# Products with the high and the low half of an input as one matmul, in three layers of an expert kernel

## The chip, the cores and the metric

One NeuronCore of a Trainium2 chip runs the whole program. The metric is device time in microseconds (us). The kernel before took 526.72 us, the median of three runs (526.52 to 526.78).

## The reference

The program is linear attention followed by a mixture of 16 experts. Only the second half matters here. Every token (4608 of them, 512 numbers each) goes to one expert, and there

```python
h = np.maximum(xg[mask_e] @ w1[g, e], 0.0)
ye = h @ w2[g, e]
out[tok_idx] = combined[:, None] * ye
```

with `w1` of 512 x 1024 and `w2` of 1024 x 512 for each of the 16 experts, all in float32. Run on the reference's inputs, the three smallest experts get 246, 238 and 217 tokens.

## The kernel before, in words

The experts are sorted by their number of tokens and worked off one after the other as regions r = 0 to 15. Tokens stand in the columns of a matmul's moving operand, weights are stationary. A region has a list of widths (`ARMS`, line 22); at run time TensorE branches to the smallest width that holds the region's tokens (`by_width`, line 337), and `CAPS` is the largest. The operations of ScalarE, VectorE and GpSimd always cover `CAPS[r]` columns, or whole groups of 32 (`groups_of`).

To keep float32 accuracy at the matmul's fast rate, every operand is split in a high part (rounded) and a low part (the rest), and a product is three matmuls (`three`, line 369): high weight by high input, high weight by low input, low weight by high input, all added up in one PSUM bank. Layer 1 of a region has 8 groups (f = 0 to 7), each of 4 chunks c by three matmuls, 96 in all; layer 2 has 4 groups (d = 0 to 3), each of 8 chunks by three, also 96. The layers of all regions follow each other on TensorE. Region 15 is the last; its layer 2 has tokens as stationary and weights as moving operand (`layer2_by_token`, line 1445) and starts with 24 matmuls of 512 columns, which read all of w2.

Around the matmuls the other engines work in an order that is written out by hand (`manual_schedule`, line 1460): each engine does its instructions strictly in the order of the code. In layer 1 of region r:

- after each group f, ScalarE takes the relu of the bank as the high part hh, and VectorE the low part hl (`split_h`, lines 324 and 325). Four banks go round, so group f + 4 waits for hl of group f;
- a quarter of w1 and four pieces of w2 are split: ScalarE rounds the high part (lines 246 and 348), VectorE subtracts for the low part (lines 250 and 352). The last quarter of w1 goes ahead of group f = 1, the pieces 0 to 3 of w2 ahead of f = 0, 2, 4 and 6 (`w1_at`, `w2_at`, line 1632);
- at f = 0, GpSimd is given the scaling of the next region's tokens (line 321, it reads and writes SBUF) and one indirect DMA for each group of 32 columns of the region before (line 1439). In region 15 these DMAs stand behind all of layer 1's code, as does `gpsimd.drain()`.

In layer 2, for each d, VectorE transposes the next region's tokens (line 311), ScalarE rounds them (line 1431), VectorE takes their low part (line 1435); three quarters of the next w1 are split (lines 246 and 250); and VectorE transposes the result of the bank psy[d] into z (line 1655).

Of the kernel before, what the change touches and what calls it, by code (L numbers as in the profile page):

```python
# [9 lines left out]
F32 = mybir.dt.float32  # L10
F32R = mybir.dt.float32r
# [3 lines left out]
ALU = mybir.AluOpType  # L15
# [5 lines left out]

ARMS = [[128], [336, 344, 360], [328, 336, 344], [312, 328], [304, 312, 328], [300, 312], [300, 304],
        [292, 300], [280, 292], [284, 292], [268, 280], [272, 280], [264, 268],
        [248, 264], [240, 260], [232, 256]]
CAPS = [arms[-1] for arms in ARMS]


# [5 lines left out]
XO = 20  # L33
XR = 18
QUICK = [0, 1, 2, 3, 4, 5, 6, 7]


PICK = 1
# [29 lines left out]
def tile_linattn_moe(ctx: ExitStack, tc: tile.TileContext, qm, qt, k, v, router, w1, w2, out):  # L68
# [179 lines left out]
    def split_low(part, h, eng):  # L248
        w, hi, lo = quarter(part, h)
        eng.tensor_tensor(out=lo, in0=w, in1=hi.bitcast(F32), op=ALU.subtract)  # L250
# [72 lines left out]
    def split_h(hh, hl, ps):  # L323
        nc.scalar.activation(out=hh, in_=ps, func=AF.Relu)  # L324
        nc.vector.scalar_tensor_tensor(out=hl, in0=ps, scalar=0.0, in1=hh.bitcast(F32), op0=ALU.max, op1=ALU.subtract)  # L325

    def layer1(ps, w1, f, xh, xl, n):
        cs = slice((f % 4) * P, (f % 4 + 1) * P)
        _, wh, wl = w1[f // 4]
        three(ps[:, 0:n], KC, lambda c: wh[:, c, cs], lambda c: wl[:, c, cs], lambda c: xh[:, c, 0:n],  # L330
              lambda c: xl[:, c, 0:n])

    def columns(r, engine):
        return nc.values_load(ncol[0:1, r:r + 1], engines=[engine], min_val=ARMS[r][0], max_val=CAPS[r],
# [2 lines left out]
    def by_width(n, choices, emit):  # L337
        if len(choices) == 1:
            emit(choices[0])
            return  # L340
        with tc.If(n <= choices[0]) as arm:
            emit(choices[0])
        with arm.Else():
            by_width(n, choices[1:], emit)
# [2 lines left out]
        hf, i2 = p // 2, p % 2  # L347
        nc.scalar.copy(out=piece(hi, hf, i2), in_=halfpiece(wt[hf][0], i2))  # L348

    def split2_low(wt, hi, lo, p):  # L350
        hf, i2 = p // 2, p % 2
        nc.vector.tensor_tensor(out=piece(lo, hf, i2), in0=halfpiece(wt[hf][0], i2),  # L352
                                in1=piece(hi, hf, i2).bitcast(F32), op=ALU.subtract)

    def piece(x, hf, i2):
        return x[:, :, :, 64 * hf + 32 * i2:64 * hf + 32 * (i2 + 1)]

    def halfpiece(w, i2):
        return w[:, :, P * i2:P * (i2 + 1)].rearrange("p c (j x) -> p c j x", x=32)
# [9 lines left out]
    def three(ps, n, stat_h, stat_l, mov_h, mov_l, lo=0, hi=None, late=0):  # L369

        hi = n if hi is None else hi
        rest = list(range(lo, lo + late))
        for c in range(lo, hi):
            nc.tensor.matmul(ps, lhsT=stat_h(c), rhs=mov_h(c), start=(c == 0), stop=False)  # L374
            nc.tensor.matmul(ps, lhsT=stat_h(c), rhs=mov_l(c), start=False, stop=False)  # L375
            if c < lo + late - 1:
                continue
            for d in rest or [c]:
                nc.tensor.matmul(ps, lhsT=stat_l(d), rhs=mov_h(d), start=False, stop=(d == n - 1))  # L379
            rest = []  # L380
# [932 lines left out]
    with ExitStack() as ph:  # L1313
# [105 lines left out]
            return idx  # L1419

        def new_x(r):
            return [mp.tile([P, KC, 384], F32R, name=nm, bufs=1)[:, :, 16 * FIRST_X[r]:] for nm in ("xh", "xl")]

        def turned(r, c):
            n = groups_of(r)
# [1 line left out]
            turn_x(xt[:, 0:32 * n], xqs[r % 2], n, c)  # L1427
            return xt

        def split_high_x(xh, xt, r, c):  # L1430
            nc.scalar.activation(out=xh[:, c, 0:CAPS[r]], in_=xt[:, 0:CAPS[r]], func=AF.Copy, scale=g2[:, 0:1])  # L1431

        def split_low_x(x, xt, r, c):
            xh, xl = (y[:, c, 0:CAPS[r]] for y in x)
            nc.vector.scalar_tensor_tensor(out=xl, in0=xt[:, 0:CAPS[r]], scalar=g2[:, 0:1], in1=xh.bitcast(F32),
                                           op0=ALU.mult, op1=ALU.subtract)

# [42 lines left out]
        HALF = KC * FF // 2  # L1480
        la = mp.tile([P, 2 * HALF], F32R, name="la", tag="w2h", bufs=1)
        lb = mp.tile([P, 2 * HALF], F32R, name="lb", tag="w2l", bufs=1)
        lc = mp.tile([P, FC * 384], F32R, name="lc", tag="hh", bufs=1)
        ld = mp.tile([P, FC * 384], F32R, name="ld", tag="hl", bufs=1)
        w1r = [(w1c[hf], *(x.rearrange("p (c f) -> p c f", c=KC) for x in y)) for hf, y in enumerate((
            (lc[:, 0:HALF], ld[:, 0:HALF]), (la[:, HALF:2 * HALF], lb[:, HALF:2 * HALF])))]
        xT, xTl = (lb[:, i * DM:(i + 1) * DM].rearrange("p (c t) -> p c t", c=KC) for i in range(2))
# [56 lines left out]
        for hf in range(2):  # L1544
            ps = bank()
            for c in range(KC):
                if hf == 1 and c == 2:
                    xts = [turned(1, i) for i in range(2)]
                    turn(0)
                    for i in range(2):  # L1550
                        split_high_x(x1[0], xts[i], 1, i)
                    split_low_x(x1, xts[0], 1, 0)
                    xts.append(turned(1, 2))
                    split_low_x(x1, xts[1], 1, 1)
                    w1n.append(half_layer(ev, 0, 1))
                three(ps, KC, lambda c: xT[:, c, :], lambda c: xTl[:, c, :], lambda c: w1r[hf][1][:, c, :],
                      lambda c: w1r[hf][2][:, c, :], lo=c, hi=c + 1)
            nc.scalar.activation(out=hr[:, hf * 512:(hf + 1) * 512], in_=ps, func=AF.Relu)
# [4 lines left out]
        turn(1)  # L1563
        xts.append(turned(1, 3))
        for i in range(2, 4):
            split_high_x(x1[0], xts[i], 1, i)
        split_low(w1n[0], 0, nc.vector)
        for i in range(2, 4):
            split_low_x(x1, xts[i], 1, i)
# [27 lines left out]
        for r in range(1, NE):  # L1597
            cap, n = CAPS[r], groups_of(r)
            last = r + 1 == NE
            xh, xl = cur  # L1600
            hh = mp.tile([P, FC, 384], F32R, name="hh", tag="hh", bufs=1)[:, :, 16 * FIRST_H[r]:]
            hl = mp.tile([P, FC, 384], F32R, name="hl", tag="hl", bufs=1)[:, :, 16 * FIRST_H[r]:]
            w2h = mp.tile([P, FC, 4, P], F32R, name="w2h", tag="w2h", bufs=1)
            w2l = mp.tile([P, FC, 4, P], F32R, name="w2l", tag="w2l", bufs=1)
            nw1 = nw2 = None
            width_r = columns(r, mybir.EngineType.PE)
            for f in range(FC):
                if f in w1_at:
                    split_piece(w1c, w1_at[f])
                if f in w2_at:  # L1610
                    split2_high(w2c, w2h, w2_at[f])
                    split2_low(w2c, w2h, w2l, w2_at[f])
                ps = bank()
                by_width(width_r, ARMS[r], lambda m: layer1(ps, w1c, f, xh, xl, m))
                split_h(hh[:, f, 0:cap], hl[:, f, 0:cap], ps[:, 0:cap])
                if r > 1:
                    next(tables, None)
                    next(tables, None)
                elif f == 4:
                    idx = indices(1)  # L1620
                if f == FC - 1 and last:
                    nc.gpsimd.drain()
                if f == 0 and not last:
                    scale(r + 1)
                    if r > 1:
                        for g in range(groups_of(r - 1)):
                            put_quarters(z, zidx, g)
                if f == 1 and not last:
                    nw1, nw2 = load_weights(eidx[0:1, r + 1:r + 2])
                if f == 2 and r + 2 < NE:  # L1630
                    pass
            w1_at, w2_at = {1: 3}, {0: 0, 2: 1, 4: 2, 6: 3}
            if last:
                for g in range(groups_of(r - 1)):
                    put_quarters(z, zidx, g)
                nc.vector.scalar_tensor_tensor(out=ridx[:, 1:3], in0=rid[:, 1:3], scalar=0.25, in1=bad[0][:, 1:3],
                                               op0=ALU.mult, op1=ALU.max)
                layer2_by_token(r, (w2h, w2l), hh, hl, ridx[:, 1:3])
                break
            z = mp.tile([P, NQ, P], F32, name="z")  # L1640
            nxt = new_x(r + 1)
            zidx = idx
            xt = [turned(r + 1, 0)]
            for d in range(4):
                split_high_x(nxt[0], xt[d], r + 1, d)
                if d < 3:
                    split_high(nw1[d // 2], d % 2)
                    xt.append(turned(r + 1, d + 1))
                    split_low(nw1[d // 2], d % 2, nc.vector)
                split_low_x(nxt, xt[d], r + 1, d)  # L1650
                ps = psy[d]
                by_width(width_r, ARMS[r], lambda m: three(
                    ps[:, 0:m], FC, lambda c: w2h[:, c, d, :], lambda c: w2l[:, c, d, :], lambda c: hh[:, c, 0:m],
                    lambda c: hl[:, c, 0:m]))
                nc.vector.transpose(z[:, 0:n, 32 * d:32 * (d + 1)], ps[:, 0:32 * n])
            idx = indices(r + 1)
            if r + 3 <= NE:
                read(r + 2) if r + 2 < NE else None
            cur, w1c, w2c = nxt, nw1, nw2
# [115 lines left out]
```

## Time and profile before

| | |
|---|---|
| median of the runs shown | 526.72 us |
| the profiled execution's own time | 526.29 us |
| its span, first to last instruction | 524.5 us |
| regions 1 to 15 on TensorE | 138.0 to 519.1 us |
| region 13, layers 1 and 2 (248 columns) | from 453.75, 464.64 us |
| region 14, layers 1 and 2 (240 columns) | from 475.51, 486.24 us |
| region 15, layers 1 and 2 (232 columns, then 512 and 256) | from 497.00, 507.71 us |

How to read it: the profile is one execution, with times from the span's start. A matmul's record shows its whole way through the engine, some 0.27 to 0.40 us, and the next one starts long before it ends, so the cost of one matmul in a stream is the distance from its start to the next start. Names such as `ps<-xl,whi` say which tile is written from which. PE is TensorE, PEld its weight loads, DVE is VectorE, ACT is ScalarE, POOL is GpSimd.

### The profile page before, as it was taken

How to read it: one execution, taken by the hardware profiler on the slowest of the kernel's cores; microseconds unless marked ns; L12 is line 12 of the kernel's file. 1: busy time of each engine (PE TensorE's matmuls, PEld its weight loads, DVE VectorE, ACT ScalarE, POOL GpSimd, SP SyncE). 2: the span in 40 equal slices, each digit the busy share in tenths (PEclk: the TensorE clock that was granted, in tenths of full speed). 3: DMA queues.
4: the chain of work that ended last, by engine and by line, in shares of the span. 5: the costliest groups of instructions: out<-in, count | busy, mean ns of one | idle time of the engine just before them, and what ended most of it. 6: DMA issues, size and time to landing. Idle time of an engine off the chain costs nothing. (4 is left out here: it accounts for less than half of the span.)

```text
span 524.5 us, 12156 instructions
## 1 busy us (share of the span) xinstructions
PE 512.8 (98%) x4258; PEld 496.4 (95%) x4262; DVE 400.9 (76%) x853; ACT 277.9 (53%) x499; POOL 258.4 (49%) x356
## 2 busy tenths in 40 slices
PE   6899999999999999999999999999999999999995
PEld 3899998689999999999999999999999999999995
DVE  4259998978888887887777777877878777878760
ACT  0377888725753544455454454545453656456451
POOL 7002865452112736647484646555564738265271
PEclk9899999999999999999999999999999999999999
DMA  8999998947897483636765656564748384864010
GB/s 319 422 422 419 418 423 345 363 176 244 263 373 311 114 322 95 267 104 196 279 232 188 230 190 242 181 262 152 280 140 318 104 335 131 305 213 179 15 40 36
DMA packets 44026, 126.50 MB, mean 241 GB/s; under 512 B 6992, under 2 KB 26390, under 8 KB 32925
## 3 DMA queue, kind: packets, MB, share of 16 engines
q1 hardware_dynamic: 36029, 105.71, 54.7%
q0 software_dynamic: 7760, 19.48, 10.0%
q8 instruction: 62, 1.02, 0.8%
q14 instruction: 31, 0.25, 0.2%
q10 hardware_dynamic: 144, 0.04, 0.0%
HBM read 105.73 MB, written 20.51 MB: 241 GB/s over the span
## 5 line engine op out<-in xcount | busy, mean ns | idle before, releaser
L1439 POOL DMA_INDIRECT out_dram<-z,idx x140 | 163.9, 1171 | 152.6 <-DVE idx L1417 105.4
L379 PE MATMUL ps<-xh,wlo 128*128 128x300 f32 (+12 forms) x480 | 141.5, 295 | 0.0
L374 PE MATMUL ps<-xh,whi 128*128 128x300 f32 (+12 forms) x480 | 141.3, 294 | 0.0
L375 PE MATMUL ps<-xl,whi 128*128 128x300 f32 (+12 forms) x480 | 141.2, 294 | 0.0
L374 PE MATMUL psy<-hh,w2h 128*128 128x300 f32 (+11 forms) x448 | 132.4, 296 | 0.0
L375 PE MATMUL psy<-hl,w2h 128*128 128x300 f32 (+11 forms) x448 | 132.4, 296 | 0.0
L379 PE MATMUL psy<-hh,w2l 128*128 128x300 f32 (+11 forms) x448 | 132.4, 295 | 0.0
L250 DVE TENSOR_TENSOR wlo<-wr,whi 128x1024 fp32r<-128x1024 f32 x64 | 97.2, 1521 | 21.2 <-ACT whi L246 21.1
L375 PEld LDWEIGHTS ps<-xl,whi 128*128 128x128 f32 x480 | 90.4, 188 | 0.0
L374 PEld LDWEIGHTS ps<-xh,whi 128*128 128x128 f32 x480 | 90.3, 188 | 0.0
L379 PEld LDWEIGHTS ps<-xh,wlo 128*128 128x128 f32 x480 | 90.3, 188 | 0.0
L324 ACT ACTIVATE hh<-ps 128x328 fp32r<-128x328 f32 (+11 forms) x120 | 50.4, 420 | 74.2 <-PE ps L379 66.9
L352 DVE TENSOR_TENSOR w2l<-wr,w2h 128x1024 fp32r<-128x1024 f32 x60 | 73.4, 1223 | 17.3 <-ACT w2h L348 16.6
L374 PEld LDWEIGHTS psy<-hh,w2h 128*128 128x128 f32 x448 | 84.2, 188 | 0.0
L375 PEld LDWEIGHTS psy<-hl,w2h 128*128 128x128 f32 x448 | 84.2, 188 | 0.0
L379 PEld LDWEIGHTS psy<-hh,w2l 128*128 128x128 f32 x448 | 84.1, 188 | 0.0
L348 ACT CAST w2h<-wr 128x1024 fp32r<-128x1024 f32 x60 | 62.5, 1042 | 37.1 <-PE psy L375 34.0
L325 DVE SCALAR_TENSOR_TENSOR hl<-ps,hh 128x328 fp32r<-128x328 f32 (+11 forms) x120 | 55.6, 464 | 21.0 <-ACT hh L324 20.9
L1431 ACT ACTIVATE xh<-xt,rw 128x328 fp32r<-128x328 f32 (+11 forms) x60 | 32.5, 544 | 67.7 <-DVE xt L311 67.7
L246 ACT CAST whi<-wr 128x1024 fp32r<-128x1024 f32 x64 | 66.2, 1037 | 0.0
L267 POOL DMA_INDIRECT xs<-xo,keys x36 | 35.7, 993 | 31.3 <-DVE pt L762 10.3
L609 PE MATMUL ops<-kvx,m_q 128*128 128x168 f32 x256 | 42.2, 315 | 0.2 <-ACT xr L552 0.2
(304 smaller groups left out, 666.8 us busy)
## 6 DMA issues: line engine op xcount, KB each, us to landing
wr<-in_w_dram SPq DMA_DIRECT2D x64, 1024.0 KB
m_q<-in_qm_dram SPq DMA_DIRECT2D x8, 1024.0 KB
m_k<-in_k_dram SPq DMA_DIRECT2D x7, 1024.0 KB
m_v<-in_v_dram SPq DMA_DIRECT2D x7, 1024.0 KB
xq<-xs SPq DMA_DIRECT2D x20, 153.0 KB
out_dram<-z,idx POOLq DMA_INDIRECT x140
xq<-xs SPq DMA_DIRECT2D x16, 136.0 KB
xq<-xs SPq DMA_DIRECT2D x12, 119.0 KB
```

The costliest lines, as they stand in the source:

```text
L246: nc.scalar.copy(out=hi, in_=w)
L250: eng.tensor_tensor(out=lo, in0=w, in1=hi.bitcast(F32), op=ALU.subtract)
L267: sc = nc.gpsimd.indirect_dma_start(out=xs, out_offset=bass.IndirectOffsetOnAxis(ap=keys[:, c:c + 1], axis=0), in_=x.rearrange("p i f -> p ...
L324: nc.scalar.activation(out=hh, in_=ps, func=AF.Relu)
L325: nc.vector.scalar_tensor_tensor(out=hl, in0=ps, scalar=0.0, in1=hh.bitcast(F32), op0=ALU.max, op1=ALU.subtract)
L348: nc.scalar.copy(out=piece(hi, hf, i2), in_=halfpiece(wt[hf][0], i2))
L352: nc.vector.tensor_tensor(out=piece(lo, hf, i2), in0=halfpiece(wt[hf][0], i2), in1=piece(hi, hf, i2).bitcast(F32), op=ALU.subtract)
L374: nc.tensor.matmul(ps, lhsT=stat_h(c), rhs=mov_h(c), start=(c == 0), stop=False)
L375: nc.tensor.matmul(ps, lhsT=stat_h(c), rhs=mov_l(c), start=False, stop=False)
L379: nc.tensor.matmul(ps, lhsT=stat_l(d), rhs=mov_h(d), start=False, stop=(d == n - 1))
L609: nc.tensor.matmul(ops[c][lo:hi, pr, 0:XW], lhsT=qs[:, pr * step_ + at + lo:pr * step_ + at + hi], rhs=kx[:, pr, :], start=True, stop=True)
L1439: sc = nc.gpsimd.indirect_dma_start(out=out4, out_offset=bass.IndirectOffsetOnAxis(ap=idx[:, g:g + 1], axis=0), in_=z[:, g, :], in_offset= ...
```

## The change

In layer 2 of regions 13 and 14 and in layer 1 of region 15 (`PAIRED`), the high weight is multiplied with the input's high and low part in one matmul of 2m columns, where m is the region's width. It writes two halves of a bank, from column 0 and from column 256; the low weight's matmul of m columns is added to the first half. The sum of the halves is then made by ScalarE, which copies the second half to SBUF, and VectorE, which adds the copy to the first half in place. In region 15 the relu and its low part of group f - 1 are issued between the copy and the addition of group f. The tiles of the high and the low input become one tile of two halves, for all regions. The last three regions' widths change: the largest is now 256, and the smaller one of region 15 is 220 (232 before). Four of VectorE's subtractions are given to GpSimd: two in `LOW_1` (w1, layer 2 of regions 13 and 14, at d = 1) and two in `LOW_2` (w2 pieces 0 and 2, region 15). Once, in region 2, the part of the four psy banks that nothing has written is set to zero.

```diff
         [292, 300], [280, 292], [284, 292], [268, 280], [272, 280], [264, 268],
-        [248, 264], [240, 260], [232, 256]]
+        [248, 256], [240, 256], [220, 256]]
 CAPS = [arms[-1] for arms in ARMS]
...
 QUICK = [0, 1, 2, 3, 4, 5, 6, 7]
+
+
+PAIRED = {(13, 2), (14, 2), (15, 1)}
+LOW_2 = {(15, 0), (15, 2)}
+LOW_1 = {(13, 1), (14, 1)}
...
-    def layer1(ps, w1, f, xh, xl, n):
+    def layer1(ps, w1, f, x, n, pair):
         cs = slice((f % 4) * P, (f % 4 + 1) * P)
         _, wh, wl = w1[f // 4]
-        three(ps[:, 0:n], KC, lambda c: wh[:, c, cs], lambda c: wl[:, c, cs], lambda c: xh[:, c, 0:n],
-              lambda c: xl[:, c, 0:n])
+        products(ps, n, KC, lambda c: wh[:, c, cs], lambda c: wl[:, c, cs], x, pair)
+
+    def products(ps, m, n, stat_h, stat_l, x, pair):
+
+        if not pair:
+            three(ps[:, 0:m], n, stat_h, stat_l, lambda c: x[:, 0, c, 0:m], lambda c: x[:, 1, c, 0:m])
+            return
+        both_parts = ps.rearrange("p (i t) -> p i t", i=2)[:, :, 0:m]
+        for c in range(n):
+            nc.tensor.matmul(both_parts, lhsT=stat_h(c), rhs=x[:, :, c, 0:m], start=(c == 0), stop=False)
+            nc.tensor.matmul(ps[:, 0:m], lhsT=stat_l(c), rhs=x[:, 0, c, 0:m], start=False, stop=(c == n - 1))
+
+    def copy_low(ps, at, cap):
+        nc.scalar.copy(out=at, in_=ps[:, 256:256 + cap])
+
+    def add_low(ps, at, cap):
+        nc.vector.tensor_tensor(out=ps[:, 0:cap], in0=ps[:, 0:cap], in1=at, op=ALU.add)
...
-    def split2_low(wt, hi, lo, p):
+    def split2_low(wt, hi, lo, p, eng):
         hf, i2 = p // 2, p % 2
-        nc.vector.tensor_tensor(out=piece(lo, hf, i2), in0=halfpiece(wt[hf][0], i2),
+        eng.tensor_tensor(out=piece(lo, hf, i2), in0=halfpiece(wt[hf][0], i2),
                                 in1=piece(hi, hf, i2).bitcast(F32), op=ALU.subtract)
...
         def new_x(r):
-            return [mp.tile([P, KC, 384], F32R, name=nm, bufs=1)[:, :, 16 * FIRST_X[r]:] for nm in ("xh", "xl")]
+            return mp.tile([P, 2, KC, 384], F32R, name="x", bufs=1)[:, :, :, 16 * FIRST_X[r]:]
...
-        def split_high_x(xh, xt, r, c):
-            nc.scalar.activation(out=xh[:, c, 0:CAPS[r]], in_=xt[:, 0:CAPS[r]], func=AF.Copy, scale=g2[:, 0:1])
+        def split_high_x(x, xt, r, c):
+            nc.scalar.activation(out=x[:, 0, c, 0:CAPS[r]], in_=xt[:, 0:CAPS[r]], func=AF.Copy, scale=g2[:, 0:1])
         def split_low_x(x, xt, r, c):
-            xh, xl = (y[:, c, 0:CAPS[r]] for y in x)
+            xh, xl = (x[:, i, c, 0:CAPS[r]] for i in range(2))
             nc.vector.scalar_tensor_tensor(out=xl, in0=xt[:, 0:CAPS[r]], scalar=g2[:, 0:1], in1=xh.bitcast(F32),
...
         lb = mp.tile([P, 2 * HALF], F32R, name="lb", tag="w2l", bufs=1)
-        lc = mp.tile([P, FC * 384], F32R, name="lc", tag="hh", bufs=1)
-        ld = mp.tile([P, FC * 384], F32R, name="ld", tag="hl", bufs=1)
+        lcd = mp.tile([P, 2, FC * 384], F32R, name="lcd", tag="h", bufs=1)
+        lc, ld = lcd[:, 0], lcd[:, 1]
         w1r = [(w1c[hf], *(x.rearrange("p (c f) -> p c f", c=KC) for x in y)) for hf, y in enumerate((
...
                     for i in range(2):
-                        split_high_x(x1[0], xts[i], 1, i)
+                        split_high_x(x1, xts[i], 1, i)
                     split_low_x(x1, xts[0], 1, 0)
...
         for i in range(2, 4):
-            split_high_x(x1[0], xts[i], 1, i)
+            split_high_x(x1, xts[i], 1, i)
         split_low(w1n[0], 0, nc.vector)
...
             last = r + 1 == NE
-            xh, xl = cur
-            hh = mp.tile([P, FC, 384], F32R, name="hh", tag="hh", bufs=1)[:, :, 16 * FIRST_H[r]:]
-            hl = mp.tile([P, FC, 384], F32R, name="hl", tag="hl", bufs=1)[:, :, 16 * FIRST_H[r]:]
+            h = mp.tile([P, 2, FC, 384], F32R, name="h", tag="h", bufs=1)[:, :, :, 16 * FIRST_H[r]:]
+            hh, hl = h[:, 0], h[:, 1]
+            pair1, pair2 = ((r, i) in PAIRED for i in (1, 2))
             w2h = mp.tile([P, FC, 4, P], F32R, name="w2h", tag="w2h", bufs=1)
...
                     split2_high(w2c, w2h, w2_at[f])
-                    split2_low(w2c, w2h, w2l, w2_at[f])
+                    split2_low(w2c, w2h, w2l, w2_at[f], nc.gpsimd if (r, w2_at[f]) in LOW_2 else nc.vector)
                 ps = bank()
-                by_width(width_r, ARMS[r], lambda m: layer1(ps, w1c, f, xh, xl, m))
-                split_h(hh[:, f, 0:cap], hl[:, f, 0:cap], ps[:, 0:cap])
+                by_width(width_r, ARMS[r], lambda m: layer1(ps, w1c, f, cur, m, pair1))
+                if pair1:
+                    low = mp.tile([P, 384], F32, name="xt", bufs=3)[:, 0:cap]
+                    copy_low(ps, low, cap)
+                    if f:
+                        split_h(*behind)
+                    add_low(ps, low, cap)
+                    behind = (hh[:, f, 0:cap], hl[:, f, 0:cap], ps[:, 0:cap])
+                    if f == FC - 1:
+                        split_h(*behind)
+                else:
+                    split_h(hh[:, f, 0:cap], hl[:, f, 0:cap], ps[:, 0:cap])
                 if r > 1:
...
             for d in range(4):
-                split_high_x(nxt[0], xt[d], r + 1, d)
+                split_high_x(nxt, xt[d], r + 1, d)
                 if d < 3:
                     xt.append(turned(r + 1, d + 1))
-                    split_low(nw1[d // 2], d % 2, nc.vector)
+                    split_low(nw1[d // 2], d % 2, nc.gpsimd if (r, d) in LOW_1 else nc.vector)
                 split_low_x(nxt, xt[d], r + 1, d)
                 ps = psy[d]
-                by_width(width_r, ARMS[r], lambda m: three(
-                    ps[:, 0:m], FC, lambda c: w2h[:, c, d, :], lambda c: w2l[:, c, d, :], lambda c: hh[:, c, 0:m],
-                    lambda c: hl[:, c, 0:m]))
+                by_width(width_r, ARMS[r], lambda m: products(
+                    ps, m, FC, lambda c: w2h[:, c, d, :], lambda c: w2l[:, c, d, :], h, pair2))
+                if pair2:
+                    low = z[:, 0:n, 32 * d:32 * (d + 1)]
+                    nc.scalar.copy(out=low, in_=ps[:, 256:256 + cap].rearrange("p (n x) -> p n x", x=32))
+                    nc.vector.tensor_tensor(out=ps[:, 0:cap].rearrange("p (n x) -> p n x", x=32),
+                                            in0=ps[:, 0:cap].rearrange("p (n x) -> p n x", x=32), in1=low, op=ALU.add)
                 nc.vector.transpose(z[:, 0:n, 32 * d:32 * (d + 1)], ps[:, 0:32 * n])
+                if r == 2:
+                    nc.vector.memset(ps[:, 384:512], 0.0)
             idx = indices(r + 1)
```

## Rows read from the trace of the kernel before

**Rows 1.** The page, part 1: busy time, share of the span and instructions of each engine

```profile
PE 512.8 (98%) x4258; PEld 496.4 (95%) x4262; DVE 400.9 (76%) x853; ACT 277.9 (53%) x499; POOL 258.4 (49%) x356
```

**Rows 2.** The waits of PE, the longest of all: us in total, times, longest

```profile
PE warm L458 <- POOL wide_b L116: 2.2, 1, 2.2
```

**Rows 3.** Busy time of each engine in three paired layers

```profile
464.60:475.50 10.90, 10.90 (x98) 10.90 (x97) 9.45 (x17) 5.17 (x8) 3.84 (x3) 1.00 0.93 352
...
486.20:497.00 10.80, 10.80 (x99) 10.80 (x99) 8.48 (x17) 5.15 (x8) 1.97 (x2) 1.00 0.04 12
...
497.00:507.70 10.70, 10.70 (x98) 10.70 (x97) 8.65 (x13) 7.45 (x12) 7.61 (x8) 1.00 0.13 40
```

**Rows 4.** Timeline of PE: start, duration; first matmuls of late layers

```profile
464.64 0.27 PE L374 MATMUL psy<-hh,w2h 128*128 128x248 f32 x1
...
475.51 0.27 PE L374 MATMUL ps<-xh,whi 128*128 128x240 f32 x1
...
486.24 0.27 PE L374 MATMUL psy<-hh,w2h 128*128 128x240 f32 x1
...
497.00 0.27 PE L374 MATMUL ps<-xh,whi 128*128 128x232 f32 x1
...
507.71 0.40 PE L374 MATMUL psy<-w2h,hh 128*128 128x512 f32 x1
...
507.95 0.42 PE L375 MATMUL psy<-w2l,hh 128*128 128x512 f32 x1
...
513.22 0.28 PE L374 MATMUL psy<-w2h,hh 128*128 128x256 f32 x1
```

**Rows 5.** Timeline of PE: first matmuls of region 1, both layers, and region 2

```profile
138.04 0.33 PE L374 MATMUL ps<-xh,whi 128*128 128x360 f32 x1
...
154.03 0.33 PE L374 MATMUL psy<-hh,w2h 128*128 128x360 f32 x1
...
169.40 0.31 PE L374 MATMUL ps<-xh,whi 128*128 128x336 f32 x1
```

**Rows 6.** Timeline of ACT in region 15

```profile
505.51 1.04 ACT L348 CAST w2h<-wr 128x1024 fp32r<-128x1024 f32 x1
...
506.57 0.39 ACT L324 ACTIVATE hh<-ps 128x256 fp32r<-128x256 f32 x1
...
516.29 0.37 ACT L1456 COPY yo<-psy 128x256 f32<-128x256 f32 x1 [2.29 <-PE psy L379]
```

**Rows 7.** Timeline of DVE in region 15, layer 1

```profile
499.95 1.23 DVE L250 TENSOR_TENSOR wlo<-wr,whi 128x1024 fp32r<-128x1024 f32 x1 [0.18 <-ACT whi L246]
...
501.09 0.42 DVE L325 SCALAR_TENSOR_TENSOR hl<-ps,hh 128x256 fp32r<-128x256 f32 x1
...
501.43 1.22 DVE L352 TENSOR_TENSOR w2l<-wr,w2h 128x1024 fp32r<-128x1024 f32 x1
...
506.59 1.23 DVE L352 TENSOR_TENSOR w2l<-wr,w2h 128x1024 fp32r<-128x1024 f32 x1 [0.51 <-ACT w2h L348]
```

**Rows 8.** Timeline of POOL and DVE where both are busy, regions 1 and 13

```profile
143.01 0.52 DVE L325 SCALAR_TENSOR_TENSOR hl<-ps,hh 128x360 fp32r<-128x360 f32 x1
...
143.02 2.57 POOL L321 TENSOR_TENSOR xq<-xq 128x1408 f32<-128x1408 f32 x1 [0.62 <-DMA xq<-xs]
...
143.44 3.23 DVE L250 TENSOR_TENSOR wlo<-wr,whi 128x1024 fp32r<-128x1024 f32 x1
...
466.82 1.94 POOL L321 TENSOR_TENSOR xq<-xq 128x1024 f32<-128x1024 f32 x1
...
467.72 2.13 DVE L250 TENSOR_TENSOR wlo<-wr,whi 128x1024 fp32r<-128x1024 f32 x1 [1.22 <-ACT whi L246]
```

**Rows 9.** Source line 1590: duration of a bank's memset, ns

```profile
L1590 DVE MEMSET psy<- x1: 112/112/112, 141.9 to 141.9; 128x64 f32 x1
```

**Rows 10.** Timeline of POOL: the last store of region 14 and the last scatter

```profile
508.96 0.97 POOL L1439 DMA_INDIRECT out_dram<-z,idx  x1 [0.30 <-issue]
...
519.81 0.97 POOL L314 DMA_INDIRECT out_dram<-yo,ridx  x1 [4.56 <-ACT yo L1456]
```

## The prediction

> **What bounds the kernel now.** I read the page's busy shares first, then TensorE's waits, then the three paired layers alone, and last the timelines of each engine there. TensorE is busy for 98% of the span [rows 1]. Its longest wait of all, 2.2 us, is for a constant of the warm-up matmuls at the start [rows 2]; it has none in regions 1 to 15, so up to region 15's last layer the time is the sum of matmul distances. The stage table shows what stands beside them: VectorE is busy for 9.45 of 10.9, 8.48 of 10.8 and 8.65 of 10.7 us in the three layers to be paired, ScalarE for 5.17, 5.15 and 7.45 [rows 3]. TensorE is the bound, but VectorE comes close behind, and in region 15 ScalarE too.
>
> One spot is closer than the shares say. The low part of the last w2 piece starts at 506.59 and takes 1.23 us [rows 7], so it lands at 507.82. The first matmul that reads a low piece starts at 507.95 [rows 4]: the margin is 0.13 us.
>
> **What the pairing takes off TensorE.** Between the first matmuls of successive layers there are 96 matmuls. Region 13's layer 2 (248 columns) takes (475.51 - 464.64)/96 = 113.2 ns each, region 14's (240) 112.1, and region 15's layer 1 (232) 111.6 [rows 4]. From 240 to 232 columns nothing but 0.5 ns is gained, where 8 columns at 2.4 GHz are 3.3 ns: a floor of about 111.6 ns lies under a matmul with a weight of its own. Over its columns at 2.4 GHz, a matmul pays 113.2 - 103.3 = 9.9 ns at 248 columns, and (513.22 - 507.71)/24 - 213.3 = 16.3 ns at 512 [rows 4]; two layers at 360 columns pay 16.6 and 10.1 [rows 5]. No row has a matmul of 440 to 496 columns into two runs. I take 13 ns, the middle, with 10 and 16 as ends.
>
> For each chunk, then, region 13 pays 206.7 + 13 + 113.2 = 332.9 ns in place of 339.6; region 14 pays 200 + 13 + 112.1 = 325.1 in place of 336.3; region 15 pays, at 220 columns (217 tokens), 183.3 + 13 + 111.6 = 307.9 in place of 334.8, since the low weight's matmul stays on the floor. Over 32 chunks each that is 0.22, 0.36 and 0.86 us: 1.44 us, with 1.7 and 1.15 at the ends.
>
> **What it adds in layer 2 of regions 13 and 14.** Each d adds a copy on ScalarE (0.37 us at 256 columns [rows 6]) and an addition on VectorE. That addition isn't in the trace; its nearest row is hl, which also reads one bank and one SBUF tile: 0.42 us [rows 7]. Its ends are 0.34 (the distance from hl to the next start, 501.09 to 501.43) and 0.52 (hl at 360 columns [rows 8]). VectorE gets four, and gives up one subtraction of 1.2 us to GpSimd. There it takes 1.94 us, as the scaling of as many elements does [rows 8]; ends 1.2 (no slower than VectorE) and 2.57 (the longest scaling row).
>
> What matters is what this does to VectorE. The low-part subtraction that began at 467.72 took 2.13 us, because GpSimd's scaling ran until 468.76; another took 3.23 us under a scaling of 2.57 us; but hl, which began at 143.01 beside the same scaling, took 0.52 [rows 8]. So a VectorE operation with two SBUF inputs waits until GpSimd is done, one with a bank and an SBUF input does not. In region 13 GpSimd now has its subtraction (from 469.3, after ScalarE's rounding) and the scaling behind it; VectorE's low part of x loses about 1 us to the first and the next subtraction 0.8 to the second, where it lost 1.04 us before. Less the removed 1.2 us, plus three additions, the last low part of x ends at 476.3; region 14's layer 1 begins at 475.3 and reads it three chunks later, at 476.4. The cover holds by 0.1 us. Region 14 has no scaling left, and holds. So region 15 begins 0.58 us earlier.
>
> **What it adds in layer 1 of region 15.** Here the new work forms a round: the addition of group f lets ScalarE take relu f, that lets VectorE take hl f, and behind it in VectorE's order stands addition f + 1. With 0.04 us from engine to engine (ScalarE's cast ends at 506.55, its user starts at 506.59 [rows 6, 7]) a round is 0.39 + 0.04 + 0.34 + 0.42 + 0.04 = 1.23 us, which is just TensorE's new time for a group (4 x 0.308). Every split that VectorE or ScalarE has in between lengthens it. I walk it from TensorE's first matmul of the layer, t = 0:
>
> ScalarE copies group 3 of region 14, then rounds piece 0 (0.47 to 1.51); GpSimd subtracts it from 1.55 to 3.49. ScalarE copies group 0 (until 1.87) and rounds the last w1 quarter (until 2.8). VectorE could subtract that at 2.85, but has two SBUF inputs and waits for GpSimd: 3.49 to 4.6. Then hl 0, addition 1 (until 5.35), piece 1 (until 6.4), hl 1, addition 2 (until 7.17). Relu 2 waited for that: 7.21. Behind it ScalarE rounds piece 2 (7.5 to 8.5), copies group 4, and takes relu 3 at 8.76; hl 3 and addition 4 end at 9.95, relu 4 starts at 9.99, and only behind it stands the rounding of piece 3, 10.27 to 11.31. VectorE subtracts piece 3 from 11.35 to 12.57, and the second matmul of layer 2 starts at 12.6. Before, it started 10.95 us after the layer's first matmul [rows 4]. TensorE alone would have come there at 10.1. The layer's gain of 0.86 us is gone, and 1.65 us are lost.
>
> After that TensorE runs through: relu 7 and hl 7 end at t = 15.4, and chunk 7 is read at 17.1. GpSimd's DMAs of region 14 now stand behind its piece 2 (t = 10.5); eight at 1.27 us (0.97 and 0.30 of issue) end 10.2 us later, at 517.2, and one other scatter fits ahead of the last, at 519.81 before [rows 10]. The four memsets in region 2, 0.11 us for 64 columns [rows 9] and at most twice that each, go to VectorE under a layer in which TensorE waits for nothing [rows 2]: nothing. The merged tiles keep the halves' order and sizes, and the narrower caps only shorten copies: nothing.
>
> **The sum.** 1.65 - 0.58 = +1.07 us, on an execution of 526.29 us; the median is 0.43 us above that: 527.8 us. With all of the unknown costs at their low ends the same walk gives no change; with all at their high ends +2.9 us.
>
> The Trainium skill (GPSIMD Engine Reference, section 3.1) gives 4497 ns for an addition of 2048 float32 elements on GpSimd; half of it, an estimate of 2.25 us, would make the sum +1.7 us, 528.4. The row's 1.94 us, from the same engine with as many elements, is what I take.
>
> **The rivals.**
> - The round doesn't bind, and TensorE stays the bound throughout: -1.44 us, 525.3. For it: up to the rounding of piece 3 ScalarE has 7.3 us of work and VectorE 6.9, in 8.1 us; only their waits for each other make it late. It decides if the last subtraction starts by t = 8.8, not 11.35. Against it: the margin was 0.13 us before anything was added. Chance 0.16.
> - GpSimd starts the scaling of region 15 right behind its subtraction in region 13, ahead of the waiting VectorE. The last low part of x comes 1.4 us too late for region 14's layer 1: +2.5 us, 529.2. No row has two such operations in line. Chance 0.12.
> - Matmuls into two runs of a bank go at half rate. 1416 columns over 32 chunks at 0.42 ns more each are +19 us, on top of the walk: 547. All outputs of the layers so far are one run, so no row speaks. Chance 0.03. The Trainium skill (PSUM - Partial Sum Buffer, Specifications) says that any non-contiguous access pattern slows matmuls significantly; no run so far shows it, and here each run is 220 columns or more.
> - The change doesn't do what it says: the wide matmul costs as much as the two, so that a chunk takes as long as before. Regions 14 and 15 then start no earlier and the walk stays, +1.7 us, 528.4; inside the range, chance 0.04 and counted with the forecast.
>
> **How the numbers follow.** Some 0.2% (1.05 us) can be told from no change here. The forecast, that the round in region 15 eats the gain, has 0.69. Its costs run from 0 to +2.9 us, with the middle just over the bound, so I split it in 0.38 slower and 0.31 within. Slower is 0.38 + 0.12 + 0.03 = 0.53, within 0.31, faster 0.16. The range goes from 525.2, which takes the faster rival in, to 529.3; it leaves out the half-rate case and the far ends. The forecast's own range is 526.7 to 529.3.
>
> **What would show it.** Right: distances of about 308 ns per chunk in region 15; layer 1 there lasting over 11 us between its first matmul and the next layer's; TensorE waiting for hl in its last groups and for `w2l` at the second matmul of layer 2; the w1 subtraction there stretched or late by GpSimd. Regions 14 and 15 starting 0.2 and 0.6 us earlier. Wrong: no such wait, or an addition well under 0.34 us, or GpSimd's subtractions not holding VectorE up; or a wait at the start of region 14, which would be the second rival.

## The result and the profile after

The changed kernel takes **532.19 us**, the median of four runs (531.75 to 532.78), beside 526.62 us (526.32 to 526.78) for the kernel before: a ratio of 1.0110, 95% interval 1.0098 to 1.0121. It is slower by 5.6 us. The forecast was 527.8 us, with a range up to 529.3: the sign is right, the size is not.

The profiled execution of the changed kernel took 531.83 us, its span 530.1 us against 524.5. The page, part 1:

```profile
PE 513.0 (97%) x4166; PEld 491.4 (93%) x4166; DVE 404.1 (76%) x869; ACT 282.3 (53%) x515; POOL 267.1 (50%) x358
```

The page counts 92 matmuls fewer than in [rows 1] (96 by the code; a trace misses some records), but TensorE is busy as long as before. Its waits, without the longest two, which the kernel before has too and which lie ahead of the experts (2.4 us for an input, 2.2 us for the warm-up of [rows 2]):

```profile
PE psy L395 <- DVE w2l L372: 0.8, 1, 0.8
PE ps L344 <- DVE h L330: 0.6, 2, 0.3
```

These two are new, both in region 15, and both on VectorE. The timeline of PE, with the first matmuls that answer to [rows 4], and the last matmul of all:

```profile
464.70 0.38 PE L344 MATMUL psy<-h,w2h 128*128 128x496 f32 x1
...
475.56 0.27 PE L394 MATMUL ps<-x,whi 128*128 128x240 f32 x1
...
486.43 0.38 PE L344 MATMUL psy<-h,w2h 128*128 128x480 f32 x1
...
496.94 0.37 PE L344 MATMUL ps<-x,whi 128*128 128x440 f32 x1
...
508.62 0.50 PE L394 MATMUL psy<-w2h,h 128*128 128x512 f32 x1
509.97 0.47 PE L395 MATMUL psy<-w2l,h 128*128 128x512 f32 x1 [0.85 <-DVE w2l L372]
...
520.93 0.28 PE L399 MATMUL psy<-w2h,h 128*128 128x256 f32 x1
```

The differences of these starts, with those of [rows 4], say where the time went:

| us | before | after |
|---|---|---|
| region 13, layer 2 (paired after) | 10.87 | 10.86 |
| region 14, layer 1 | 10.73 | 10.87 |
| region 14, layer 2 (paired after) | 10.76 | 10.51 |
| region 15, from the first matmul of layer 1 (paired after) to the second of layer 2 | 10.95 | 13.03 |
| from there to the last matmul | 10.90 | 10.96 |
| last matmul to the end of the span | 5.64 | 9.20 |

So the 5.6 us are in the main two things of different kinds: 2.1 us on TensorE in region 15, and 3.6 us behind TensorE's last matmul, where the forecast had nothing. For the second the timeline of POOL is the view to read:

```profile
469.41 2.39 POOL L255 TENSOR_TENSOR wlo<-wr,whi 128x1024 fp32r<-128x1024 f32 x1 [2.53 <-DMA wr<-in_w_dram]
471.76 2.09 POOL L326 TENSOR_TENSOR xq<-xq 128x1024 f32<-128x1024 f32 x1
...
498.54 2.42 POOL L372 TENSOR_TENSOR w2l<-wr,w2h 128x1024 fp32r<-128x1024 f32 x1 [4.93 <-ACT w2h L368]
505.93 2.40 POOL L372 TENSOR_TENSOR w2l<-wr,w2h 128x1024 fp32r<-128x1024 f32 x1 [4.98 <-ACT w2h L368]
514.43 0.99 POOL L1459 DMA_INDIRECT out_dram<-z,idx  x1 [6.09 <-DVEq L1704]
...
524.67 0.97 POOL L319 DMA_INDIRECT out_dram<-yo,ridx  x1 [0.30 <-DMA out_dram<-z,idx]
525.95 0.98 POOL L319 DMA_INDIRECT out_dram<-yo,ridx  x1 [0.30 <-DMA out_dram<-z,idx]
```

The first two rows are region 13's, for later. GpSimd is done with piece 2 at 508.33 and issues its first store of region 14 only at 514.43. From there eight stores and two scatters follow each other with only the 0.30 us of issue between them. The 6.09 us of idle time are put down to VectorE's queue; the row that fills most of them is `gpsimd.drain()` in GpSimd's own queue (duration in ns, then the start), first after, then before:

```profile
L1652 POOLq DRAIN  x1: 7672/7672/7672, 505.9 to 505.9; - x1
```

```profile
L1622 POOLq DRAIN  x1: 13243/13243/13243, 480.5 to 480.5; - x1
```

After, the drain ends at 505.9 + 7.67 = 513.6, which is 5.2 us after the subtraction ended. Before, it ended at 480.5 + 13.24 = 493.7, and the last GpSimd work ahead of it was this store, ended at 488.47:

```profile
487.50 0.97 POOL L1439 DMA_INDIRECT out_dram<-z,idx  x1 [0.30 <-issue]
```

Again 5.2 to 5.3 us, but in a stretch in which GpSimd had nothing else to do until 497.96.

### The profile page after: what moved, and what is told of

It is laid out like the page before. It is cut to its first block, busy times and chain, and to the rows that moved or that the text cites. A ratio compares the mean times of both kernels' runs of the same rounds, so it can differ in the third digit from the quotient of the medians.

```text
span 530.1 us, 12029 instructions
## 1 busy us (share of the span) xinstructions
PE 513.0 (97%) x4166; PEld 491.4 (93%) x4166; DVE 404.1 (76%) x869; ACT 282.3 (53%) x515; POOL 267.1 (50%) x358
## 4 chain that ended last, share of the span: by engine, by line
PE 81%; DMA 11%; issue 3%; DVE 2%; POOL 1%; POOLq 1%; SPq 0%; ACT 0%
PE ps L399 12%; PE ps L394 12%; PE ps L395 12%; PE psy L395 10%; PE psy L394 10%; PE psy L399 10%; DMA tail_k<-in_k_dram 3%; DMA tail_v<-in_v_dram 3%; DMA m_v<-in_v_dram 3%; PE psy L344 3%; PE l L383 3%; PE ops L629 2%; PE l L1290 2%; PE kps L583 1%; PE psy L345 1%
## 5 line engine op out<-in xcount | busy, mean ns | idle before, releaser
L399 PE MATMUL ps<-x,wlo 128*128 128x300 f32 (+11 forms) x448 | 132.8, 296 | 0.0
L394 PE MATMUL ps<-x,whi 128*128 128x300 f32 (+11 forms) x448 | 132.7, 296 | 0.0
L395 PE MATMUL ps<-x,whi 128*128 128x300 f32 (+11 forms) x448 | 132.5, 296 | 0.0
L394 PE MATMUL psy<-h,w2h 128*128 128x300 f32 (+9 forms) x384 | 114.9, 299 | 0.0
L395 PE MATMUL psy<-h,w2h 128*128 128x300 f32 (+9 forms) x384 | 114.9, 299 | 0.0
L399 PE MATMUL psy<-h,w2l 128*128 128x300 f32 (+9 forms) x384 | 114.8, 299 | 0.0
L329 ACT ACTIVATE h<-ps 128x256 fp32r<-128x256 f32 (+9 forms) x120 | 50.4, 420 | 75.5 <-PE ps L399 64.7
L395 PEld LDWEIGHTS ps<-x,whi 128*128 128x128 f32 x448 | 84.3, 188 | 0.0
L394 PEld LDWEIGHTS ps<-x,whi 128*128 128x128 f32 x448 | 84.2, 188 | 0.1
L399 PEld LDWEIGHTS ps<-x,wlo 128*128 128x128 f32 x448 | 84.1, 188 | 0.0
L330 DVE SCALAR_TENSOR_TENSOR h<-ps,h 128x256 fp32r<-128x256 f32 (+9 forms) x120 | 55.3, 462 | 23.3 <-ACT h L329 23.2
L394 PEld LDWEIGHTS psy<-h,w2h 128*128 128x128 f32 x384 | 72.1, 188 | 0.0
L395 PEld LDWEIGHTS psy<-h,w2h 128*128 128x128 f32 x384 | 72.1, 188 | 0.0
L399 PEld LDWEIGHTS psy<-h,w2l 128*128 128x128 f32 x384 | 72.1, 188 | 0.0
```

## The experiments

The theory for the tail was that the drain pays its 5.2 us behind whatever GpSimd did last; the rival, that the stores are late only because they stand behind piece 2. For region 15 the theory was the round of the forecast, ScalarE and VectorE waiting for each other; the rival, that GpSimd's subtractions hold VectorE up and without them the round is harmless. For TensorE's small gain the question was whether the gap between the two halves of a bank costs anything, against a matmul that pays more over its columns when it is wide. Where the expectations use letters, A is the drain, C the round, D GpSimd's subtractions and E the gap.

**A first set of four** met a chip on which the kernel before itself took 594 to 616 us and the four edits took medians of 597.6 to 607.6. In the trace of the edit below TensorE waited 13.4 and 10.2 us in all for the rounded and the low pieces of w2. These times tell nothing of the edits, which were run again. The one usable reading is behind the last matmul, where no weights are loaded. The drain is moved ahead of region 15's layer 1, and the same edit was then timed again (the second expectation):

```diff
+            if last:
+                nc.gpsimd.drain()
...
-                if f == FC - 1 and last:
-                    nc.gpsimd.drain()
```

> GpSimd's drain stands ahead of the two pieces of w2 in region 15 instead of behind them; nothing else differs from the changed kernel. Theory A (the drain): in the changed kernel's trace the drain ends 5.2 us after GpSimd's last subtraction, and the eight stores of region 14 and the two scatters queue behind it, so the kernel ends about 3.6 us after TensorE would let it. With the drain first, the stores begin at about 508.5 and the time falls to about 528.6 us; TensorE's end stays 2.0 us later than before. Rival (the stores themselves are slow, or the late TensorE alone makes the end late): 531.5 us or more.

> The kernel with the drain first once more, since the first time weights arrived late in all kernels alike (the kernel before took 607.6 us there). As expected then: theory A (the drain's 5.2 us and the stores behind it end the kernel late): about 528.6 us, TensorE's end still 2.0 us later than before. Rival: 531.5 us or more. The first time the span ended 5.5 us after TensorE's last matmul began, 9.2 us in the changed kernel, which speaks for A.

In the first set: 605.52 us, ratio 1.0107 (0.9965 to 1.0248), and 5.49 us from the last matmul to the end. Run again: **529.13 us**, ratio 1.0044 (1.0027 to 1.0061), 3.1 us less than the changed kernel. The timeline of POOL:

```profile
499.59 2.40 POOL L372 TENSOR_TENSOR w2l<-wr,w2h 128x1024 fp32r<-128x1024 f32 x1 [5.48 <-ACT xt L348]
506.98 2.40 POOL L372 TENSOR_TENSOR w2l<-wr,w2h 128x1024 fp32r<-128x1024 f32 x1 [4.99 <-ACT w2h L368]
509.54 0.99 POOL L1459 DMA_INDIRECT out_dram<-z,idx  x1 [0.16 <-DVE ps L351]
...
519.77 0.97 POOL L319 DMA_INDIRECT out_dram<-yo,ridx  x1 [0.30 <-ACT yo L1476]
522.91 0.97 POOL L319 DMA_INDIRECT out_dram<-yo,ridx  x1 [2.17 <-ACT yo L1476]
```

The same two subtractions stand ahead of the same eight stores, but the first store starts 0.16 us behind the second subtraction instead of 6.09, and the last scatter waits for its data again. From the last matmul (521.95) to the end it is 5.44 us. The tail was the drain, not the queue's length; and 529.13 us lies inside the range of the forecast. The move has a price of its own: the drain now ends at 491.7 + 7.66 = 499.4 and holds GpSimd's first subtraction, which starts 2.13 us after the layer's first matmul instead of 1.60; region 15 takes 13.55 us to the second matmul instead of 13.03.

**Without GpSimd's subtractions in region 15** (VectorE does all four):

```diff
-LOW_2 = {(15, 0), (15, 2)}
+LOW_2 = set()
```

> The kernel with the two w2 pieces back on VectorE once more. Theory C (ScalarE and VectorE wait for each other in region 15): TensorE ends 1.6 to 2.0 us later than before, 528.2 to 528.6 us in all. Rival D (GpSimd's slow subtractions are what makes region 15 late): 526.9 us at most.

Measured 528.26 us, ratio 1.0027 (1.0017 to 1.0036). The tail is back at 5.64 us, with the drain where the change has it: GpSimd's last work ahead of the drain ends at 493.87, and the first store starts again 6.09 us behind it, now at 499.96, where it holds nothing up. The layer hardly moves: 12.77 us from its first matmul (497.21) to the second of layer 2.

```profile
508.72 0.50 PE L394 MATMUL psy<-w2h,h 128*128 128x512 f32 x1
509.98 0.50 PE L395 MATMUL psy<-w2l,h 128*128 128x512 f32 x1 [0.76 <-DVE w2l L372]
```

Giving the two pieces back to VectorE takes 0.26 us net off the 2.08. With the subtractions off GpSimd the layer is late all the same, so they alone are not what makes it late.

**Layer 1 of region 15 not paired**, at the new width of 220 columns, and VectorE with all pieces:

```diff
-PAIRED = {(13, 2), (14, 2), (15, 1)}
-LOW_2 = {(15, 0), (15, 2)}
+PAIRED = {(13, 2), (14, 2)}
+LOW_2 = set()
```

> Pairing in layer 2 of regions 13 and 14 alone, once more. As the prediction had it: 526.0 us. As the changed kernel's trace has it (region 13 gains nothing, region 14 gains 0.25 us, 0.14 us are lost in a wait at the start of region 14): 526.5 us, no change.

Measured 526.23 us, ratio 0.9988 (0.9979 to 0.9998). What is left of the change, the pairings of regions 13 and 14 above all, is worth 0.12%. TensorE's part of it is smaller: from region 1's first matmul to the last of all it takes 380.71 us, before 380.81, 0.10 us less. The layer's first matmul and the next layer's:

```profile
497.13 0.27 PE L394 MATMUL ps<-x,whi 128*128 128x220 f32 x1
...
507.85 0.40 PE L394 MATMUL psy<-w2h,h 128*128 128x512 f32 x1
```

10.72 us for 96 matmuls of 220 columns, 111.7 ns each; 232 columns took 111.6 [rows 4]. The floor of the forecast is there: the narrower width alone gives nothing.

**The round shortened**: the drain ahead as above, and the addition of group f ahead of the relu of group f - 1, so that VectorE doesn't take it behind hl:

```diff
                     copy_low(ps, low, cap)
+                    add_low(ps, low, cap)
                     if f:
                         split_h(*behind)
-                    add_low(ps, low, cap)
```

> As the kernel with the drain first, with VectorE's addition of group f ahead of the relu and the low part of group f - 1, once more. Theory C (the round relu, low part, addition, relu is the bound): 0.7 us less than with the drain first alone, about 527.9 us. Rival D (the amount of work, or GpSimd's slow subtractions): no change against the drain first alone.

Measured 528.44 us, ratio 1.0030 (1.0020 to 1.0041). 12.83 us to the second matmul, 0.72 less than the 13.55 with the drain's move alone, with the same work on every engine. What is left shows in two waits: 0.38 us for piece 3, where the drain's move alone had 0.86, and 1.5 us for a bank, where it had 1.1; the bank now waits for ScalarE's relu instead of hl:

```profile
509.09 0.40 PE L394 MATMUL psy<-w2h,h 128*128 128x512 f32 x1
509.88 0.47 PE L395 MATMUL psy<-w2l,h 128*128 128x512 f32 x1 [0.38 <-DVE w2l L372]
```

```profile
PE ps L344 <- ACT h L329: 1.5, 2, 1.1
```

**No sum at all in region 15.** TensorE's paired matmuls stay, copies and additions are left out, so that the product of the input's low part is missing from layer 1 there:

```diff
-LOW_2 = {(15, 0), (15, 2)}
+LOW_2 = set()
...
-                if pair1:
+                if False:
```

> As the kernel with the w2 pieces back on VectorE, but region 15 leaves out the copy and the addition of the two halves: the product of the high weight with the low input is computed and not used there. That shows what the pairing of layer 1 is worth to TensorE alone. Theory C (the sum's two operations and their round make the layer late): the layer's 32 chunks take 309 ns each, 9.9 us in place of 11.5, its second matmul of layer 2 comes 10.2 us after the layer's first, and the time is 0.7 us under the kernel before the change less what regions 13 and 14 give, 525.5 us. Rival (TensorE itself is slower with paired matmuls beside so many splits): the layer stays over 11 us, 527.5 us or more.

Measured 525.95 us, ratio 0.9987 (0.9977 to 0.9996).

```profile
497.06 0.37 PE L344 MATMUL ps<-x,whi 128*128 128x440 f32 x1
...
507.20 0.40 PE L394 MATMUL psy<-w2h,h 128*128 128x512 f32 x1
507.54 0.50 PE L395 MATMUL psy<-w2l,h 128*128 128x512 f32 x1
```

10.14 us for the layer, where its 32 chunks were forecast at 32 x 0.308 = 9.85. Against the 12.77 us with the sum it is 2.3 us less to the second matmul: eight copies at 0.38 us and eight additions at 0.42, some 6.4 us of work on two engines that were not full, cost TensorE that. This run takes away the work and the round together, so it does not say which of them it was. What TensorE gains at most in this layer is 0.6 us, not 0.86.

**The halves in one run.** In regions 13 and 14 the second half starts right behind the first, at column 248 or 240 in place of 256 (copy and addition follow, and the larger width is dropped):

```diff
-        [248, 256], [240, 256], [220, 256]]
+        [248], [240], [220, 256]]
...
-        both_parts = ps.rearrange("p (i t) -> p i t", i=2)[:, :, 0:m]
+        both_parts = (ps[:, 0:2 * m] if m in (240, 248) else ps).rearrange("p (i t) -> p i t", i=2)[:, :, 0:m]
```

> In layer 2 of regions 13 and 14 the second half of the bank begins at column m instead of 256, so that the wide matmul writes one run of 496 or 480 columns; all else in these layers is as in the changed kernel, and GpSimd's pieces and drain in region 15 too, so the total stays near 532 us. Theory E (a gap in the output costs): a wide matmul takes 225 ns over two runs in region 13, 18 ns over its columns; over one run it falls to 217 ns or less, the layer from 10.86 to 10.6 us. Rival (the gap costs nothing, the wide matmul has that much over its columns anyway, as one of 512 columns has 16 ns): 223 to 225 ns, 10.8 us.

Measured 531.68 us, ratio 1.0098 (1.0081 to 1.0115), as the changed kernel.

```profile
464.70 0.38 PE L344 MATMUL psy<-h,w2h 128*128 128x496 f32 x1
...
475.57 0.27 PE L394 MATMUL ps<-x,whi 128*128 128x240 f32 x1
```

Region 13's layer 2 takes 10.87 us in one run and 10.86 in two, and a wide matmul 224.4 ns from its start to the next against 224.5. The gap costs nothing, so the wide matmul itself is dearer than I took.

**A version that keeps the gain.** The drain and the addition ahead, w2 pieces 1 to 3 split at groups 1, 3 and 5 instead of 2, 4 and 6, GpSimd with pieces 1 and 2, and region 13 not paired:

```diff
-PAIRED = {(13, 2), (14, 2), (15, 1)}
-LOW_2 = {(15, 0), (15, 2)}
-LOW_1 = {(13, 1), (14, 1)}
+PAIRED = {(14, 2), (15, 1)}
+LOW_2 = {(15, 1), (15, 2)}
+LOW_1 = set()
...
+            if last:
+                w2_at = {0: 0, 1: 1, 3: 2, 5: 3}
```

> A version meant to be faster than both: pairing in layer 2 of region 14 and layer 1 of region 15, w1 splits all on VectorE, the addition of group f ahead of relu f - 1, drain ahead of GpSimd's work, and the w2 pieces of region 15 split ahead of f = 0, 1, 3 and 5 with pieces 1 and 2 on GpSimd. By theory C, walked with GpSimd's measured 2.4 us, the last piece then lands before TensorE reads it by 0.2 us at most, TensorE ends 0.85 us earlier than before, 525.8 us. Rival D (the amount of work in region 15 is the bound): 527 us or more.

Measured **525.78 us**, ratio 0.9984 (0.9974 to 0.9994): 0.8 us faster than the kernel before, which had 526.55 us beside it, and some 6 us faster than the changed one.

```profile
137.62 0.33 PE L394 MATMUL ps<-x,whi 128*128 128x360 f32 x1
...
496.32 0.36 PE L344 MATMUL ps<-x,whi 128*128 128x440 f32 x1
...
506.44 0.40 PE L394 MATMUL psy<-w2h,h 128*128 128x512 f32 x1
506.68 0.39 PE L395 MATMUL psy<-w2l,h 128*128 128x512 f32 x1
...
517.55 0.28 PE L399 MATMUL psy<-w2h,h 128*128 128x256 f32 x1
```

This execution began region 1 by 0.42 us earlier than that of the kernel before (138.04 [rows 5]), so only distances compare: 379.93 us from region 1's first matmul to the last of all, before 380.81, which is 0.88 less where 0.85 was expected. The low part of piece 3 is there in time, the second matmul follows 0.24 us behind the first as in [rows 4], and the layer takes 10.12 us, as long as with no sum at all. In it VectorE and ScalarE are busy for 8.9 and 8.8 us, in the changed kernel for 9.1 and 8.7: the amount of work is about the same, so rival D, here the amount of work, is out. The drain has returned into GpSimd's free time (it ends at 491.9), since GpSimd has no subtraction in region 14.

**The last w1 quarter earlier.** The same, with that quarter split at the end of region 14's layer 2, ahead of region 15:

```diff
-                w2_at = {0: 0, 1: 1, 3: 2, 5: 3}
+                w1_at, w2_at = {}, {0: 0, 1: 1, 3: 2, 5: 3}
...
                 split_low_x(nxt, xt[d], r + 1, d)
+                if d == 3 and r + 2 == NE:
+                    split_piece(nw1, 3)
```

> As the kernel with the pieces early, and the last w1 quarter of region 15 split at the end of region 14's layer 2 instead of in region 15. Theory C: hardly more than that kernel gives, 525.7 us, since the last piece is already in time. Rival D: a split less in region 15 takes 1 us off whatever the kernel with the pieces early takes.

Measured 525.81 us, ratio 0.9989 (0.9979 to 0.9999): no difference to the version above. The layer took 10.30 us, so a split less did not shorten it.

## Why the prediction missed

**The failed step** is this one: "GpSimd's DMAs of region 14 now stand behind its piece 2 (t = 10.5); eight at 1.27 us ... end 10.2 us later, at 517.2, and one other scatter fits ahead of the last". It reckoned the stores and left out the drain, which the code puts between piece 2 and the stores. That is **3.6 us of the 4.5 us** by which the sum fell short (5.6 measured against 1.07), and by itself takes the time out of the range. The text ahead of the prediction names the drain beside the stores; the walk gave it no time. With the drain out of the way the step holds: in the run with the drain ahead the stores follow piece 2 at once, one scatter goes ahead, and the last waits for ScalarE, not for the queue. The price could be read before: the drain's row and the end of the store ahead of it are both in that trace. It cost nothing there because GpSimd was idle for 9.49 us ahead of region 14's stores, and the question for a moved instruction, what cover it leaves, was asked of the stores and not of what stood between them.

The other three misses make 0.9 us:

- **What TensorE gains.** A wide matmul was taken at 13 ns over its columns. From the distances in the changed kernel, 32 of each: 224.5 ns at 496 columns (17.8 over) and 216.6 at 480 (16.6); at 440 columns in the version that keeps the gain 213.7 (30). The low weight's matmul of 248 columns behind it takes 115.0 ns. 224.5 + 115.0 is 339.5 ns for a chunk of region 13, three matmuls before were 339.9: almost nothing of the 0.22 us came. Region 14 gained 0.25 of 0.36 us. In region 15 the pairing gives at most 0.6 of 0.86 us. The rival that the wide matmul costs as much as the two was true of region 13 alone.
- **The start of region 14's layer 1.** GpSimd's subtraction took 2.39 us, not 1.94, held VectorE's low part of x from 470.43 for 1.65 us, and the last low part ended at 476.54, forecast 476.3. "The cover holds by 0.1 us" was right of the first matmul that reads it, which started at 476.68 without a gap, but the layer took 10.87 us, 0.14 more than before. The loss lies right behind, between groups 0 and 1, where TensorE branches to the width; three distances take 0.48 us instead of 0.34 (rows below). The layer took 10.72 us in the version that keeps the gain, where the low part is there before the layer begins, and 10.72 with the halves in one run, where region 14 has one width and no branch. That the late low part holds the branch up is thus likely; no run tests it alone. With this and the smaller gains region 15 began 0.06 us earlier than before (0.12 counted from region 1's first matmul), not 0.58.
- **GpSimd's subtraction**, 2.40 to 2.42 us in region 15 as well, where I took the scaling's 1.94 [rows 8]. The prediction's other estimate, 2.25 us, was half of the figure that the Trainium skill (GPSIMD Engine Reference, section 3.1) gives for an addition of 2048 float32 elements; the trace is nearer to that than to the row. The longer subtraction moves everything behind the w1 quarter by 0.4 to 0.5 us.

TensorE's rows for the second of these:

```profile
476.68 0.28 PE L395 MATMUL ps<-x,whi 128*128 128x240 f32 x1
...
476.96 0.37 PE L394 MATMUL ps<-x,whi 128*128 128x240 f32 x1
477.16 0.28 PE L395 MATMUL ps<-x,whi 128*128 128x240 f32 x1
```

**The walk through region 15 held.** It forecast 1.65 us lost there, and 2.08 were. Here are VectorE's and ScalarE's timelines of the changed kernel, in this order (the first two rows of VectorE's are region 13's, for the wait above):

```profile
470.43 1.65 DVE L1455 SCALAR_TENSOR_TENSOR x<-xt,rw,x 128x256 fp32r<-128x256 f32 x1
...
476.09 0.45 DVE L1455 SCALAR_TENSOR_TENSOR x<-xt,rw,x 128x256 fp32r<-128x256 f32 x1
...
499.87 2.16 DVE L255 TENSOR_TENSOR wlo<-wr,whi 128x1024 fp32r<-128x1024 f32 x1 [0.52 <-ACT whi L251]
501.95 0.41 DVE L330 SCALAR_TENSOR_TENSOR h<-ps,h 128x256 fp32r<-128x256 f32 x1
502.29 0.42 DVE L351 TENSOR_TENSOR ps<-ps,xt 128x256 f32<-128x256 f32 x1
502.62 1.21 DVE L372 TENSOR_TENSOR w2l<-wr,w2h 128x1024 fp32r<-128x1024 f32 x1
...
504.08 0.42 DVE L351 TENSOR_TENSOR ps<-ps,xt 128x256 f32<-128x256 f32 x1
...
506.45 0.42 DVE L330 SCALAR_TENSOR_TENSOR h<-ps,h 128x256 fp32r<-128x256 f32 x1 [0.73 <-ACT h L329]
506.79 0.42 DVE L351 TENSOR_TENSOR ps<-ps,xt 128x256 f32<-128x256 f32 x1
...
508.60 1.22 DVE L372 TENSOR_TENSOR w2l<-wr,w2h 128x1024 fp32r<-128x1024 f32 x1 [0.17 <-ACT w2h L368]
```

```profile
504.54 0.38 ACT L329 ACTIVATE h<-ps 128x256 fp32r<-128x256 f32 x1 [1.15 <-DVE ps L351]
504.82 1.04 ACT L368 CAST w2h<-wr 128x1024 fp32r<-128x1024 f32 x1
...
507.25 0.39 ACT L329 ACTIVATE h<-ps 128x256 fp32r<-128x256 f32 x1 [0.57 <-DVE ps L351]
507.53 1.04 ACT L368 CAST w2h<-wr 128x1024 fp32r<-128x1024 f32 x1
```

The w1 quarter's low part starts at 499.87 and is done only after GpSimd's subtraction (498.54 to 500.96): 2.16 us instead of 1.23. Behind it stand hl, addition, piece 1, hl, addition; relu 2 waits 1.15 us for that addition, and the rounding of piece 2 stands behind relu 2. Relu 4 waits 0.57 us, the rounding of piece 3 stands behind it, and its low part ends at 509.82, t = 12.88 from the layer's first matmul; forecast 12.57. Each step of the walk is 0.3 to 0.5 us later than written, about what GpSimd's longer subtraction brings. With the drain ahead, the shortened round took 0.72 us off with the same work, and the version with the pieces split earlier, again with the same work, took all of the lateness. So it is shown that the order in which VectorE and ScalarE wait for each other makes region 15 late, and not the amount of work. How much of the 2.08 us is the round of addition, relu and low part, and how much the rounding of pieces 2 and 3 that stands behind it, no run separates.

**The rest.** The additions start 0.33 us before the next operation and take 0.42, as hl did; the floor is confirmed. The memsets and the merged tiles cost nothing: from region 1's first matmul to region 13's it is 315.71 us in both kernels. Of the rivals, the round that doesn't bind (525.3) did not come with the change as it stands; in the rearranged version, without region 13's pairing, it doesn't bind, and the time is 525.78. GpSimd's scaling did start at 471.76, right behind its subtraction in region 13, but VectorE's waiting low part of x ended at 472.08, not behind the scaling, and the 2.5 us did not come. Half rate in two runs did not come either. The Trainium skill (PSUM - Partial Sum Buffer, Specifications) says that any non-contiguous access pattern slows matmuls significantly; for two runs of 248 columns each the trace shows no difference to one run of 496 (224.5 against 224.4 ns for a matmul).

## What to carry to other kernels

Before an instruction is given to an engine that looks idle, list what its queue does next, drains and other bookkeeping included, and read from the old trace how long each lasted behind its last work; idle time that hides a cost of 5 us is not free. Two engines that pass a tile to and fro make a round whose length can set the pace while neither is full: order the code so that the operation which feeds the other engine goes first, and move long splits out of the last rounds. A merged matmul can save next to nothing (224.5 ns for two that took 226.6 at 248 columns, 216.6 for 224.2 at 240), so measure it at the widths of the layer before building a sum around it.

## What the hardware showed that I had not expected

- A drain on GpSimd ended 5.2 to 5.3 us after the last work ahead of it in all ten traces other than those of the first set, whether that was a subtraction (508.33 to 513.6) or an indirect DMA's issue (488.47 to 493.7); what stands behind it in GpSimd's queue waits.
- GpSimd's subtraction of 1024 float32 elements in each partition takes 2.40 us, 0.46 more than its scaling of as many [rows 8].
- A low weight's matmul of 220 columns behind a wide one of 440 takes 102 ns from start to start in the version that keeps the gain, under the 111.7 ns of the same width in a stream of equal ones; the wide one gives most of it back, with 214 ns for 183 ns of columns at 2.4 GHz. No run tests why.
